# A list scheduler's figure for the speed of transfers: 280 bytes per ns in place of 240

## The chip, the core and the metric

One core of a Trainium2 chip runs the kernel. The metric is the device time of one execution in microseconds, and a lower time is better. TensorE (PE) does the matrix products, VectorE (DVE) and ScalarE (ACT) the elementwise work, GpSimd (POOL) and SyncE (SP) issue the transfers between the chip's main memory and its on-chip memory. Each engine works through its own instructions in the order in which they were written; an instruction whose input isn't there holds up all that stands behind it on that engine.

## What is computed

Attention with a compressed memory, and behind it a feed-forward layer with a squared relu, all in fp32 accuracy.

```python
a = softmax(phi, axis=2)                       # phi: 8 batches, 8 heads, 576 rows, 32 columns
k_m = einsum('bhsm,bhsd->bhmd', a, k)          # 32 memory rows of 64 numbers for each head
v_m = einsum('bhsm,bhsd->bhmd', a, v)
attn = softmax(q @ k_m.T / sqrt(64))           # 576 x 32 for each head
x = (attn @ v_m), heads side by side           # 4608 tokens x 512
g = relu(x @ w_in) ** 2                        # w_in 512 x 2048
out = g @ w_out                                # w_out 2048 x 512
```

## The kernel before

Every number that enters a product is split into a high and a low part, and a product is three products of parts. v_m is multiplied into w_in ahead of time, so that x is never formed: for each batch b and each of 16 slices of 128 columns of the hidden layer there is a step g (128 steps). **mm1** (L740) multiplies the attention with the prepared slice ("vw") into h; ACT or DVE apply the relu (L744, L745) and the square (L746 gives the high part gh, L748 the full square); DVE subtracts (L750) to get the low part **glo**. **mm2** adds gh (L770, L771) and then glo (L773) times w_out ("wo") into four accumulators.

The first 180 us also hold work that is done once. The 16 slices of w_in and w_out, two halves each, come encoded; `decode` turns a half into its parts. For each of these 32 halves it issues a load of 512 KB, **raw** (L322, on SP's queue), DVE reads that in L324 and L326 and goes on with L327, L328, L340 or L342, L344 and L357, ACT works in between (L325 and a copy), and for the first slices PE subtracts in L350, L351 and L352, of which the last needs what L340 wrote. POOL stores the parts of w_in to memory (L364), and adds the low part of w_out by a transfer (L361); `wi_again` loads the parts of w_in once more for other batches (L369). A raw buffer is loaded again when DVE has read it for the last time (L340 or L342). `memory` loads k, v and phi of four heads of a batch (L377, L378; two buffers of KV), makes the softmax of phi, and forms k_m and v_m on PE (**pkv**, L426). `scores` (L557 loads q, L569 transposes it on DVE) and `first_attention` (for batches 0 and 1; scores on PE in L636, back to rows in L664 and L671, low parts on DVE in L668) make the attention; its softmax is L682 to L688 on DVE.

The order of all of it is not written out by hand. `Plan.order` is a list scheduler: each operation has a duration for each engine that can do it, a list of what it must wait for, and, if it is a transfer, a size in bytes. A backward pass gives each operation a latest start; a forward pass fills the engines, always with the most urgent operation that is ready on the engine that is free first, and keeps one clock for all transfers, `wire`. Operations marked `lead` count as 9000 ns more urgent. The schedule sets the order on each engine (and, for a few operations that two engines can do, the engine). Where its times are off, the order stays, and the engine waits in that order. A transfer's time in the schedule is made so:

```python
wire = max(wire, t + 600) + o.size / WIRE
o.end = wire + LANDS[e]          # LANDS: 1400 ns for SP, 4000 for POOL
```

The size of a raw load is 4096 * 128 = 524,288 bytes.

Of the kernel before, what the change touches and what calls it, by code (L numbers as in the profile page):

```python
# [24 lines left out]

STEP = 5200
LANDS = {"SP": 1400, "POOL": 4000}
WIRE = 240.0
LEAD = 9000


# [21 lines left out]
class Plan:  # L53
# [56 lines left out]

    def order(self):
        for o in reversed(self.ops):
            cost = min(o.ways.values()) + o.lat + o.size / WIRE + (1800 if o.size else 0)
            late = min((u.late for u in o.users), default=1e9)
            if o.cap is not None:
                late = min(late, o.cap)
            o.late = late - cost
        for o in self.ops:
            o.left, o.ready = len(o.deps), 0.0
        free = {"PE": 0.0, "DVE": 0.0, "ACT": 0.0, "POOL": 0.0, "SP": 0.0}  # L120
        wire = 0.0
        port = {"DVE": 0.0, "POOL": 0.0}
        waiting = {e: [] for e in free}
        ready = {e: [] for e in free}

        def add(o):
            for e in o.ways:
                heapq.heappush(waiting[e], (o.ready, o.seq, o))

        for o in self.ops:  # L130
            o.start = None
            if not o.left:
                add(o)
        out = []
        while len(out) < len(self.ops):
            best = None
            for e in free:
                w, q = waiting[e], ready[e]
                while w and (w[0][0] <= free[e] or w[0][2].start is not None):
                    _, _, o = heapq.heappop(w)  # L140
                    if o.start is None:
                        heapq.heappush(q, (o.late - (LEAD if o.lead else 0), o.seq, o))
                while q and q[0][2].start is not None:
                    heapq.heappop(q)
                if q:
                    t = free[e]
                elif w:
                    t = w[0][0]
                else:
                    continue  # L150
                if best is None or t < best[0]:
                    best = t, e
            t, e = best
            free[e] = max(free[e], t)
            w, q = waiting[e], ready[e]
            while w and w[0][0] <= free[e]:
                _, _, o = heapq.heappop(w)
                if o.start is None:
                    heapq.heappush(q, (o.late - (LEAD if o.lead else 0), o.seq, o))
            while q and q[0][2].start is not None:  # L160
                heapq.heappop(q)
            if not q:
                continue
            _, _, o = heapq.heappop(q)
            t = free[e]
            d = o.ways[e]
            if o.port.get(e):
                other = "POOL" if e == "DVE" else "DVE"
                t = max(t, port[other])
                port[e] = t + d  # L170
            o.start, o.left = t, e
            free[e] = t + d
            o.end = t + d + o.lat
            if o.size:
                wire = max(wire, t + 600) + o.size / WIRE
                o.end = wire + LANDS[e]
            out.append(o)
            for u in o.users:
                u.left -= 1
                u.ready = max(u.ready, o.end)  # L180
                if not u.left:
                    add(u)
        out.sort(key=lambda o: (o.start, o.seq))
        return out
# [752 lines left out]
```

## Time and profile before

| | us |
|---|---|
| median of 3 timed runs | 819.76 |
| lowest and highest of these | 812.38 and 821.96 |
| the profiled execution's own time | 816.34 |
| its span, first to last instruction | 814.6 |

The profiled execution has 1.7 us outside its span, and its time lies inside the three timed ones. The mean granted TensorE clock is 0.994 of full speed. In rows of the profile, "idle" in square brackets is how long an engine had stood still before an instruction, and behind the arrow is what ended that.

### The profile page before, as it was taken

To read this page: it belongs to the slowest core of one execution; us is meant where nothing else is said; L and a number is where in the kernel's file an instruction comes from. 1 tells how busy PE (TensorE), PEld (TensorE's weight loads), DVE (VectorE), ACT (ScalarE), POOL (GpSimd) and SP (SyncE) were. 2 spreads that over 40 slices of the span, in tenths; PEclk is the share of its full clock that TensorE was granted. 3 is DMA by queue.
4 is the path that set the end of the run, shared out by engine and by line. 5 is a ranking of instruction groups with operands and counts; after the bars stand their busy time and mean duration, and the time that the engine had idled before them with its cause. 6 is when DMAs were issued, how large, how long until landed. Compare 5 with 4: busy or idle time off the path is not lost.

```text
span 814.6 us, 13267 instructions
## 1 busy us (share of the span) xinstructions
PE 776.2 (95%) x4926; PEld 652.5 (80%) x4926; DVE 536.4 (66%) x1190; ACT 403.1 (49%) x922; POOL 63.8 (8%) x103
## 2 busy tenths in 40 slices
PE   4889999999999999999999999999999999999995
PEld 2567888778887888888778888888788888888884
DVE  4678888783468976766776556877677556864540
ACT  2557766675653465634445355644334355643220
POOL 4012202320100100010000100010000100000000
PEclk9999999999999999999999999999999999999998
DMA  7969967666456523423443433513422433100001
GB/s 225 270 191 286 270 176 239 188 170 191 125 146 189 165 81 105 129 37 90 132 125 88 126 106 104 136 34 91 133 58 70 122 108 104 30 24 29 1 1 64
DMA packets 99716, 101.04 MB, mean 124 GB/s; under 512 B 32260, under 2 KB 85508, under 8 KB 99652
## 3 DMA queue, kind: packets, MB, share of 16 engines
q1 hardware_dynamic: 89188, 81.55, 34.2%
q0 software_dynamic: 10464, 18.65, 8.8%
q8 instruction: 39, 0.64, 0.3%
q14 instruction: 25, 0.20, 0.1%
HBM read 79.17 MB, written 17.83 MB: 119 GB/s over the span
## 4 chain that ended last, share of the span: by engine, by line
PE 73%; DVE 8%; issue 6%; DMA 5%; ACT 4%; SPq 1%; POOL 1%; DVEq 0%; POOLq 0%; ACTq 0%
PE h L740 20%; PE acc L770 12%; PE acc L773 12%; PE acc L771 12%; PE accl L796 5%; PE pvw L536 4%; PE psc L574 3%; PE pkv L426 2%; DMA raw<-in_moe_w_out_dram 1%; DMA phi<-in_phi_dram 1%; ACT vw L260 1%; DMA raw<-in_moe_w_in_dram 1%; DMA wo<-work 1%; DVE glo L750 1%; DVE work L327 1%
## 5 line engine op out<-in xcount | busy, mean ns | idle before, releaser
L740 PE MATMUL h<-ath,vw 128*128 128x320 f32 (+1 forms) x1024 | 211.6, 298 | 1.1 <-ACT r L744 0.6
L770 PE MATMUL acc<-wo,gh 128*128 128x512 f32 x512 | 207.0, 404 | 1.8 <-ACT gh L746 1.6
L771 PE MATMUL acc<-wo,gh 128*128 128x512 f32 x512 | 201.7, 394 | 0.0
L740 PEld LDWEIGHTS h<-ath,vw 128*128 128x128 f32 x1024 | 171.0, 189 | 17.2 <-ACT r L744 1.7
L773 PE MATMUL acc<-wo,glo 128*128 128x512 f32 x512 | 162.1, 405 | 1.7 <-DVE glo L750 1.5
L260 ACT CAST vw<-pvw 64x256 fp32r<-64x256 f32 (+1 forms) x224 | 85.7, 397 | 74.5 <-PE pvw L536 35.4
L545 DVE TENSOR_TENSOR vw<-pvw,vw 64x256 fp32r<-64x256 f32 x192 | 78.8, 420 | 64.8 <-ACT vw L260 62.9
L770 PEld LDWEIGHTS acc<-wo,gh 128*128 128x128 f32 x512 | 96.4, 188 | 23.4 <-ACT gh L746 3.7
L740 PE MATMUL h<-atl,vw 128*128 128x320 f32 (+1 forms) x512 | 109.9, 295 | 0.0
L771 PEld LDWEIGHTS acc<-wo,gh 128*128 128x128 f32 x512 | 96.4, 188 | 16.6
L773 PEld LDWEIGHTS acc<-wo,glo 128*128 128x128 f32 x512 | 89.5, 189 | 19.5 <-DVE glo L750 6.2
L746 ACT ACTIVATE gh<-r 128x512 fp32r<-128x512 f32 x128 | 80.8, 632 | 43.4 <-DVE r L745 37.6
L750 DVE TENSOR_TENSOR glo<-r,gh 128x512 fp32r<-128x512 f32 x128 | 87.5, 684 | 21.4 <-ACT r L748 19.7
L744 ACT ACTIVATE r<-h 128x256 f32<-128x256 f32 (+1 forms) x149 | 60.1, 406 | 56.8 <-PE h L740 53.5
L745 DVE TENSOR_SCALAR r<-h 128x320 f32<-128x320 f32 (+1 forms) x107 | 48.9, 459 | 58.4 <-PE h L740 57.9
L740 PEld LDWEIGHTS h<-atl,vw 128*128 128x128 f32 x512 | 82.5, 189 | 0.7 <-issue 0.2
L747 ACT ACTIVATE gl<-r 128x64 fp32r<-128x64 f32 x128 | 32.8, 256 | 68.5 <-DVE r L745 66.5
L748 ACT ACTIVATE r<-r 128x576 f32<-128x576 f32 x94 | 64.5, 686 | 2.2
L796 PE MATMUL accl<-wo,gl 128*128 128x512 f32 x192 | 52.3, 397 | 0.1
L796 PEld LDWEIGHTS accl<-wo,gl 128*128 128x128 f32 x192 | 35.0, 188 | 7.2 <-DVE o L260 0.5
L536 PE MATMUL pvw<-wi,VTh 128*128 128x256 f32 x192 | 37.3, 286 | 0.6 <-issue 0.3
L749 DVE TENSOR_TENSOR r<-r 128x576 f32<-128x576 f32 x34 | 25.7, 756 | 15.8 <-ACT gh L746 14.4
(137 smaller groups left out, 854.3 us busy)
## 6 DMA issues: line engine op xcount, KB each, us to landing
wi<-w_in_hi SPq DMA_DIRECT2D x56, 256.0 KB
wi<-w_in_lo SPq DMA_DIRECT2D x56, 256.0 KB
KV<-in_k_dram SPq DMA_DIRECT2D x32, 256.0 KB
KV<-in_v_dram SPq DMA_DIRECT2D x32, 256.0 KB
raw<-in_moe_w_in_dram SPq DMA_DIRECT2D x16, 512.0 KB
raw<-in_moe_w_out_dram SPq DMA_DIRECT2D x16, 512.0 KB
q<-in_q_dram SPq DMA_DIRECT2D x24, 288.0 KB
out_dram<-o POOLq DMA_DIRECT2D x20, 256.0 KB, 7.7
```

What stands on the lines that cost most here:

```text
L260: nc.scalar.copy(o, i) if e == "ACT" else ENG[e].tensor_copy(o, i)
L536: nc.tensor.matmul(pw()[:, x * SL:(x + 1) * SL], l()[:, 2 * hh + x, :], w(r, x), start=(i == 0), stop=(i == 2))
L545: vec({"DVE": tt(SL)}, lambda e, V=V, pr=pr, src=src: nc.vector.tensor_sub(V()[pr, 1, hh, :], src(), V()[pr, 0, hh, :].bitcast(F32)), [pw, ...
L740: nc.tensor.matmul(p()[:, 0:n], V()[:, l, hh, c0:c0 + P], x()[:, hh, cs], start=(i == 0), stop=(i == 5))
L744: op({"ACT": act(n) - 30, **({} if b < 2 else {"DVE": tt(n)})}, lambda e, cs=cs, n=n, p=p: nc.scalar.activation(r()[:, cs], p()[:, 0:n], A ...
L746: op({"ACT": act(SM)}, lambda e: nc.scalar.activation(gh(), r()[:, 0:SM], AF.Square), [r], [gh])
L748: op({"ACT": act(S), **({} if b < 2 else {"DVE": tt(S)})}, lambda e: nc.scalar.activation(r(), r(), AF.Square) if e == "ACT" else nc.vecto ...
L750: vec({"DVE": tt(SM)}, lambda e: nc.vector.tensor_sub(glo(), r()[:, 0:SM], gh().bitcast(F32)), [r, gh], [glo])
L770: nc.tensor.matmul(a(), gh()[:, c], t()[:, 0], start=f0, stop=False)
L771: nc.tensor.matmul(a(), gh()[:, c], t()[:, 1], start=False, stop=False)
L773: nc.tensor.matmul(a(), glo()[:, c], t()[:, 0], start=False, stop=f1)
L796: nc.tensor.matmul(a(), G()[:, l, :], t()[:, w], start=(ff == 0 and n == 0), stop=(ff == NFF - 1 and n == 2))
```

## The change

The one figure becomes two: 240 for transfers that the forward pass places in the first 30,000 ns of its own time, 280 for those after, and 280 for all in the backward pass. No operation is added or removed, no buffer and no size changes.

```diff
-WIRE = 240.0
+WIRE = (240.0, 280.0)
...
-            cost = min(o.ways.values()) + o.lat + o.size / WIRE + (1800 if o.size else 0)
+            cost = min(o.ways.values()) + o.lat + o.size / WIRE[1] + (1800 if o.size else 0)
...
-                wire = max(wire, t + 600) + o.size / WIRE
+                wire = max(wire, t + 600) + o.size / WIRE[t > 30000]
```

A raw load is 2185 ns of the scheduler's wire at 240 and 1872 at 280. What it does to the program is another order: on PE some 256 of its 1629 runs of like instructions stand elsewhere, 11 of 283 transfers on SP's queue, 3 of 94 on POOL's; 68 operations go from ACT to DVE or back (DVE has 10 more, ACT 10 fewer). The first difference lies near 37 us of the time before; most lie between 60 and 290, some between 340 and 450 and between 540 and 650; the last 150 us are the same.

**SP's queue, near 62 us.** KV_1_1 holds half of k and v of batch 1, and raw is the load of half a slice of w_in. Before:

```order
L377 DMA KV_1_1_631<-in_k_dram 128x2x256
L378 DMA KV_1_1_631<-in_k_dram 64x2x64
L377 DMA KV_1_1_631<-in_v_dram 128x2x256
L378 DMA KV_1_1_631<-in_v_dram 64x2x64
L322 DMA raw<-in_moe_w_in_dram 128x2x512
```

and now:

```order
L377 DMA KV_1_1_633<-in_k_dram 128x2x256
L378 DMA KV_1_1_633<-in_k_dram 64x2x64
L322 DMA raw<-in_moe_w_in_dram 128x2x512
L377 DMA KV_1_1_633<-in_v_dram 128x2x256
L378 DMA KV_1_1_633<-in_v_dram 64x2x64
```

The raw load has gone ahead of the two loads of v.

**DVE, near 86 us.** glo_1004 and glo_1005 are step 3's, wi_3_1 is half a slice of w_in that is being decoded, L324 begins the decoding of a half of w_out, and red and S belong to the softmax of batch 1. Before:

```order
L750 TENSOR_TENSOR glo_1004<-r_950,gh_971 128x512
L328 TENSOR_SCALAR work<-work 128x512
L682 TENSOR_REDUCE red_0_1012<-S_0_1002 128x16
L340 SCALAR_TENSOR_TENSOR wi_3_1_1006<-raw,work 128x512
L324 TENSOR_SCALAR work<-raw 128x512
L326 TENSOR_SCALAR work<-raw 128x512
L683 TENSOR_TENSOR S_0_1002<-S_0_1002,red_0_1012 128x512
```

and now:

```order
L750 TENSOR_TENSOR glo_1005<-r_956,gh_977 128x512
L328 TENSOR_SCALAR work<-work 128x512
L324 TENSOR_SCALAR work<-raw 128x512
L340 SCALAR_TENSOR_TENSOR wi_3_1_953<-raw,work 128x512
L326 TENSOR_SCALAR work<-raw 128x512
L751 TENSOR_TENSOR gl_992<-r_956,gl_992 128x64
L327 SCALAR_TENSOR_TENSOR work<-work 128x512
```

L324 now stands ahead of L340 of wi_3_1, and the softmax has gone behind (its L682 is 7 rows further on).

**PE at the same place.** psc are the scores of batch 1, pd is what decoding puts on PE. Before:

```order
L350 MATMUL pd_0_998<-work,ident 128x512
L636 MATMUL psc_0_973<-kbd_0_652,qT_0_859 128x64 x8
L351 MATMUL pd_0_998<-wi_3_0_968,minus 128x512
L352 MATMUL pd_0_998<-wi_3_0_968,minus 128x512
L770 MATMUL acc_0_3_617<-wo_686,gh_971 128x512
L771 MATMUL acc_0_3_617<-wo_686,gh_971 128x512
L636 MATMUL psc_1_1021<-kbd_1_842,qT_1_907 128x64 x8
L350 MATMUL pd_1_1038<-work,ident 128x512
L351 MATMUL pd_1_1038<-wi_3_1_1006,minus 128x512
L352 MATMUL pd_1_1038<-wi_3_1_1006,minus 128x512
L773 MATMUL acc_0_0_555<-wo_686,glo_1004 128x512
```

and now:

```order
L352 MATMUL pd_0_947<-wi_3_0_900,minus 128x512
L613 MATMUL pq_1_1_966<-ident,q_1_386 128x128 x4
L740 MATMUL h_1_1081<-ath_449,vw_0_2_889 128x320 x2
L350 MATMUL pd_1_987<-work,ident 128x512
L351 MATMUL pd_1_987<-wi_3_1_953,minus 128x512
L622 MATMUL pql_996<-ident,qx_427 128x128 x2
L352 MATMUL pd_1_987<-wi_3_1_953,minus 128x512
L773 MATMUL acc_0_0_555<-wo_662,glo_1005 128x512
L773 MATMUL acc_0_1_606<-wo_662,glo_1005 128x512
L740 MATMUL h_0_1095<-ath_449,vw_0_2_889 128x256
L636 MATMUL psc_0_1019<-kbd_0_658,qT_0_876 128x64 x4
```

Both blocks of psc stood ahead of L352 of wi_3_1, and now stand behind it.

**DVE, near 133 us.** glo_1545 and glo_1534 are step 10's, glo_1570 is step 11's, and the last L324 in the first piece reads the load for a half of w_out. Before:

```order
L328 TENSOR_SCALAR work<-work 128x512
L342 SCALAR_TENSOR_TENSOR work<-raw,work 128x512
L324 TENSOR_SCALAR work<-raw 128x512
L750 TENSOR_TENSOR glo_1545<-r_1506,gh_1522 128x512
L751 TENSOR_TENSOR gl_856<-r_1506,gl_856 128x64
L344 TENSOR_TENSOR work<-work 128x512
```

and now:

```order
L327 SCALAR_TENSOR_TENSOR work<-work 128x512
L750 TENSOR_TENSOR glo_1534<-r_1479,gh_1512 128x512
L751 TENSOR_TENSOR gl_940<-r_1479,gl_940 128x64
L328 TENSOR_SCALAR work<-work 128x512
L342 SCALAR_TENSOR_TENSOR work<-raw,work 128x512
L750 TENSOR_TENSOR glo_1570<-r_1536,gh_1546 128x512
L344 TENSOR_TENSOR work<-work 128x512
L751 TENSOR_TENSOR gl_992<-r_1536,gl_992 128x64
L324 TENSOR_SCALAR work<-raw 128x512
```

The low parts of steps 10 and 11 stood behind that L324, and now stand ahead of it.

## Rows read from the trace of the kernel before

**Rows 1.** The profile page, busy time of each engine.

```profile
PE 776.2 (95%) x4926; PEld 652.5 (80%) x4926; DVE 536.4 (66%) x1190; ACT 403.1 (49%) x922; POOL 63.8 (8%) x103
```

**Rows 2.** The page, the chain that ended last, by engine.

```profile
PE 73%; DVE 8%; issue 6%; DMA 5%; ACT 4%; SPq 1%; POOL 1%; DVEq 0%; POOLq 0%; ACTq 0%
```

**Rows 3.** Busy us in five stretches; last PEclk, DMA share, GB/s.

```profile
0.00:60.00 60.00, 41.95 (x405) 28.52 (x406) 36.24 (x85) 27.59 (x56) 13.74 (x26) 0.97 0.81 228
60.00:130.00 70.00, 68.07 (x467) 56.23 (x466) 59.15 (x128) 50.41 (x108) 14.76 (x20) 1.00 0.84 250
130.00:200.00 70.00, 64.75 (x383) 56.24 (x382) 49.94 (x99) 46.60 (x100) 14.32 (x18) 1.00 0.66 189
200.00:260.00 60.00, 59.42 (x453) 48.73 (x453) 33.57 (x80) 30.31 (x70) 3.51 (x9) 1.00 0.53 149
260.00:815.00 555.00, 542.02 (x3227) 462.77 (x3225) 357.48 (x801) 248.15 (x590) 17.49 (x31) 0.99 0.30 86
```

**Rows 4.** The same columns, 20 us each, where transfers are densest.

```profile
60.00:80.00 20.00, 19.57 (x171) 14.80 (x170) 16.19 (x37) 13.83 (x30) 3.48 (x7) 1.00 0.90 288
80.00:100.00 20.00, 20.00 (x130) 16.68 (x129) 18.19 (x39) 15.93 (x35) 6.36 (x8) 1.00 0.92 260
```

**Rows 5.** Waits of PE, 60 to 200 us: total us, times, longest.

```profile
PE pvw L516 <- ACT vw L260: 2.0, 2, 1.6
PE acc L770 <- ACT gh L746: 1.6, 2, 0.9
PE patl L671 <- DVE atl L668: 1.5, 1, 1.5
PE acc L773 <- DVE glo L750: 1.3, 1, 1.3
PE pd L352 <- DVE wi L340: 0.4, 1, 0.4
```

**Rows 6.** Waits of DVE for transfers, the same stretch and columns.

```profile
DVE work L324 <- DMA wo<-work: 6.3, 3, 3.1
...
DVE work L324 <- DMA raw<-in_moe_w_out_dram: 3.5, 3, 1.4
...
DVE work L324 <- DMA raw<-in_moe_w_in_dram: 1.5, 3, 0.8
```

**Rows 7.** Timeline near 62 us: start, us, engine, line.

```profile
62.17 0.64 SPq L377 DMA_DIRECT2D KV<-in_v_dram  x1
...
64.50 0.37 SPq L322 DMA_DIRECT2D raw<-in_moe_w_in_dram  x1
...
69.32 0.54 PE L426 MATMUL pkv<-KV,phi 128*32 128x128 f32 x12
```

**Rows 8.** Timeline of SP, PE and DVE, 81 to 91 us.

```profile
81.83 3.77 SPq L322 DMA_DIRECT2D raw<-in_moe_w_out_dram  x2
...
84.85 1.96 PE L636 MATMUL psc<-kbd,qT 128*128 128x64 f32 x16
...
86.61 0.48 PE L351 MATMUL pd<-wi,minus 128*128 128x512 f32 x1
...
87.63 1.89 PE L636 MATMUL psc<-kbd,qT 128*128 128x64 f32 x16
88.07 0.68 DVE L340 SCALAR_TENSOR_TENSOR wi<-raw,work 128x512 fp32r<-128x512 uint32 x1
...
89.43 0.55 DVE L324 TENSOR_SCALAR work<-raw 128x512 f32<-128x512 f32 x1 [0.68 <-DMA raw<-in_moe_w_out_dram]
...
90.50 0.39 PE L352 MATMUL pd<-wi,minus 128*128 128x512 f32 x1
```

**Rows 9.** Timeline of PE, 108 to 111 us.

```profile
109.13 0.33 PE L671 MATMUL patl<-ident,S 128*128 128x128 f32 x1 [1.49 <-DVE atl L668]
```

**Rows 10.** Timeline of DVE, 128 to 136 us.

```profile
133.78 0.43 DVE L324 TENSOR_SCALAR work<-raw 128x512 f32<-128x512 f32 x1 [1.44 <-DMA raw<-in_moe_w_out_dram]
134.12 0.68 DVE L750 TENSOR_TENSOR glo<-r,gh 128x512 fp32r<-128x512 f32 x1
```

**Rows 11.** Timeline of PE at the same place.

```profile
134.86 0.73 PE L773 MATMUL acc<-wo,glo 128*128 128x512 f32 x2 [1.33 <-DVE glo L750]
```

**Rows 12.** Timeline of SP, DVE and PE, 184 to 199 us.

```profile
185.06 0.55 SPq L557 DMA_DIRECT2D q<-in_q_dram  x1
...
190.13 0.69 DVE L750 TENSOR_TENSOR glo<-r,gh 128x512 fp32r<-128x512 f32 x1 [0.83 <-ACT r L748]
...
192.75 0.60 SPq L557 DMA_DIRECT2D q<-in_q_dram  x1
...
196.71 0.71 DVE L569 STREAM_TRANSPOSE qT<-q 128x512 f32<-128x512 f32 x1 [4.33 <-DMA q<-in_q_dram]
...
198.34 0.62 PE L773 MATMUL acc<-wo,glo 128*128 128x512 f32 x2
```

## The prediction

> **What bounds the kernel now.** I began with the busy time of each engine: PE is busy for 776 of 815 us, DVE for 66%, ACT for 49% [rows 1]. The chain that ended last agrees, with PE on 73% of it [rows 2]. A share over the whole span hides stages, so the table of five stretches came next [rows 3]. Before 60 us PE stands for 60.00 - 41.95 = 18.1 us. Then it stands for 1.9 us up to 130, 5.3 us from 130 to 200, 0.6 us from 200 to 260, and 13.0 us in the 555 us after that. After 60 us, then, PE is the bound by its work, and the change leaves that work as it is: the same products, in another order. A new order can only take away PE's waits or make new ones. There are 7.2 us of PE idle between 60 and 200 us to take away. A new wait there costs its full length, since later stretches have too little idle time in which to make it up.
>
> Who holds PE up in that stretch is in the waits: ACT with vw (2.0 us) and gh (1.6), DVE with atl (1.5), glo (1.3) and L340 (0.4) [rows 5]. DVE in turn stood 11.3 us at L324, the first reader of a raw load or of a buffer that a transfer must free (6.3 + 3.5 + 1.5) [rows 6]. Only 1.3 us of that came through to PE, in a place that I come to below.
>
> Is the new figure nearer the truth? Where transfers are densest they moved 288 and 260 GB/s at a busy share of 0.90 and 0.92 [rows 4], which divided by the share is 320 and 283. As a rate of the whole, 280 describes this better than 240. But the schedule needs something else: when one load is there. A raw load of 524,288 bytes is 2.2 us of its wire at 240 and 1.9 at 280, plus 0.6 before and 1.4 behind, so 4.2 and then 3.9 us if nothing is ahead of it. The load issued at 81.83 was waited for until 89.43, which is 7.6 us [rows 8]. At that place the old figure was already too hopeful, and the new one is more so.
>
> **The change, place by place.** All sums are against the profiled execution, 816.34 us.
>
> *Near 62 us, SP.* The raw load moves ahead of the two loads of v. It waited for a buffer until 64.50, so the loads of v that began at 62.17 now begin at 64.87: 2.7 us later [rows 7]. PE used them at 69.32 without idle time of its own, so they had landed by then; how long before, these rows don't say. The cost to PE is 0 to 2.7 us. Which value it is doesn't matter much, because the next place swallows it.
>
> *Near 88 us, DVE and PE.* L324 of the next half of w_out now stands ahead of L340 of wi_3_1. In the trace L324 could only start at 89.43, when its load was there, while L340 had gone at 88.07 [rows 8]. The load is issued when DVE frees its buffer, and that part of DVE's row keeps its place, so I keep 89.43. L340 then starts behind L324's 0.55 us and takes 0.68: it ends at 90.66. On PE, L352 needs L340's result. In the trace PE came to it at 90.50 with two blocks of scores ahead of it; they took 86.61 - 84.85 = 1.76 and 89.36 - 87.63 = 1.73 us [rows 8]. Both are now behind, so PE comes to L352 at 90.50 - 3.49 = 87.01 and waits until 90.66: **+3.6 us**, and a delay from 62 us shortens this wait by as much as it lasted. The bounds are 0 (the load comes 3.6 us sooner, since its buffer is free sooner) and +4.5 (the load shares its time with more others). I take 3.6, since it is built on the rows of this very load.
>
> *95 to 115 us.* The scores of batch 1 come later, and with them the softmax and the return to rows (L671). PE's wait there, 1.5 us [rows 9], was a wait for atl at a time when DVE had too much to do. PE now comes 3.6 us later with more filler ahead (steps 5 to 7 and the next slices of vw move up), in the new order that chain stands behind four to five us more of DVE's work; the two about match, so I count the wait as gone: **-1.5**, bounds -1.5 and +2. The low part of step 4 stands behind a further L324, whose load is issued late by the same lag; I add **+0.5**, bounds 0 and +3 (the 3.1 us that was the longest wait of an L324 [rows 6]).
>
> *Near 133 us, DVE.* The low part of step 10 stood behind an L324 that waited 1.44 us for its load, and PE waited 1.33 us for that low part [rows 10, 11]. It now stands ahead of the L324: **-1.3**, bounds -1.3 and 0. What is late next there is L344 behind the same L324, which feeds the decoding and not PE.
>
> *Near 190 us, DVE.* L569, which waits for q, moves ahead of the low part of step 20. It stood 4.3 us for q in the trace, the second part of which was issued at 192.75; this part now goes directly behind the first, at about 185.6 [rows 12]. At the 4.0 us or less that it took (192.75 to 196.71) it is there at 189.6, and at the 7.6 that the raw load of rows 8 took, at 193.2. L569 (0.7), a maximum of about twice that, and the subtraction itself (0.7) then put the low part of step 20 at 196.0 at the latest. PE needs it at 198.34 [rows 12]. The cover is 2.3 us, so **0**; without it, up to +2.
>
> *The rest.* The waits for ACT, 3.6 us in all [rows 5], may go or double: 0, bounds -3.6 and +3.6. After 200 us steps of `memory` for batches 2 to 4 move 6 to 10 us of PE's work ahead, in a stretch where PE stands for 0.6 us [rows 3]; it is filler that changes places: 0, bounds -3 and +3.
>
> The sum is 3.6 - 1.5 + 0.5 - 1.3 = +1.3, so 817.6 for an execution like the profiled one. The median of the timed runs lies 3.4 us above that execution and would give 821.1. Three runs that spread over 9.6 us don't say which is the better zero, so I take the middle: **819 us**.
>
> The Trainium skill, page "DMA: Bandwidth & Descriptors", section "Queues, rings and completion order", says that each of the 16 engines takes turns, packet by packet, between all queues that have work for it. By this rule no single queue of transfers with one rate tells when a load lands, since a load is stretched by whatever POOL and SP have under way beside it, and a hopeful figure puts DVE in front of an absent load again and again. The trace agrees at one place: 524,288 bytes in 7.6 us are 69 bytes per ns for this load [rows 8], while all transfers together moved 260 GB/s [rows 4]. By the figure of the schedule (3.9 us) the place near 88 us would cost nothing and the sum would be 814 us; by the rule it costs 3.6 or more, and the first rival below is its general form.
>
> **The rivals.**
>
> *Slower.* DVE works in order, and each L324 that comes ahead of its load holds up the low parts, L340 and softmaxes behind it. Some 22 raw loads are still to come after 60 us. If the block of 88 us came at five more of them, at about 2.7 us each that come through to PE, that is 3.6 + 13.5 - 2.8 = +14.3: 831 us. It decides where DVE has less other work between an L324 and its load than the load is late. For it: DVE is busy for 18.19 of 20 us near 90 us [rows 4], so it can't catch up there, and loads took 7.6 us. Against it: of 11.3 us that DVE stood at L324, PE felt 1.3 [rows 5, 6], because PE has mostly other work queued.
>
> *Faster.* 280 is the truer rate, waits go and few come: the 7.2 us of PE idle between 60 and 200 shrink to nothing, 816.34 - 7.2 = 809 us. For it: the rate [rows 4], and two waits that I see going. Against it: the waits for ACT are no matter of transfers. More than 2% would need the 18 us before 60 us as well, and there the order is nearly the same until 37 us.
>
> *Nothing.* The order differs, but PE is the bound and the differences are filler: 816 to 820 us. It is told from my forecast by the trace alone: no new wait at L352 near 88 us, and the one at 134.86 still there.
>
> **How the numbers follow.** My forecast, gain and loss that nearly cancel, gets 0.38; nothing 0.28; the faster rival 0.22; the slower one 0.12. The range takes 808 (just under the faster rival) and 831 (the slower one), and leaves out some 0.1 at each side for the bounds that add up (-1.5 - 1.3 - 3.6 - 3 gives 807; 4.5 + 2 + 3 + 3.6 on 819.76 gives 833). Two per cent, about what a measurement of this kernel can tell from no change, is 16.4 us: below 803 or above 836. The faster rival comes that far only with part of the first 60 us, 0.05; the slower one with seven or more such blocks, 0.09; the rest, 0.86, lies within.
>
> **What would show it.** In the changed kernel's profile, PE should wait 2 to 4 us at L352 near 88 to 91 us with L340 named, and L324 should be idle for a raw load just ahead of that. The wait of L671 near 109 should be gone or below 0.5 us, and so should that of L773 for glo near 135. pkv near 69 us should begin later or wait. L569 should follow q at 190 to 193 us, and PE shouldn't wait for glo there. PE's idle time from 200 us on should be what it was. I am wrong if the load is there by 86 us (then 814 or less), or if several L324 hold PE up between 95 and 180 us (then 826 or more).

## The result, and the profile after

The changed kernel's median is 822.36 us (820.57 to 830.84, 20 runs) against 817.89 (812.38 to 823.83, 20 runs) for the kernel before on the same chip: ratio 1.0073, 95% interval 1.0044 to 1.0103. The ratio goes by the means of the runs, which lie 6.0 us apart; the medians lie 4.5 apart. That is within 2%, as forecast, but it is a loss of 4.5 to 6 us, clear of noise, and not the +1.3 of the sum. The profiled execution took 822.78 us, its span 821.0; before it was 816.34 and 814.6.

The page of the changed kernel, busy time and the chain by engine [rows 1, 2]:

```profile
PE 779.0 (95%) x4926; PEld 654.9 (80%) x4926; DVE 542.4 (66%) x1200; ACT 397.8 (48%) x912; POOL 63.4 (8%) x103
...
PE 71%; DVE 9%; issue 7%; DMA 6%; ACT 3%; POOL 1%; SPq 1%; DVEq 0%; POOLq 0%; ACTq 0%
```

PE was idle for 814.6 - 776.2 = 38.4 us before and for 821.0 - 779.0 = 42.0 now: 3.6 us of the 6.4 between the spans are new idle time, and 2.8 are the same 4926 matmuls at longer times. The chain agrees: PE 71% in place of 73%, the difference at DVE, DMA and issue. Not all of the 6.4 us can come from the change: ahead of 37 us, where the first row differs, the changed kernel's execution is already 1.4 us behind, as the first block of scores shows (before, then now):

```profile
26.80 2.00 PE L636 MATMUL psc<-kbd,qT 128*128 128x64 f32 x16
```

```profile
28.21 2.00 PE L636 MATMUL psc<-kbd,qT 128*128 128x64 f32 x16
```

The stretches of [rows 3] and the 20-us windows of [rows 4], in the changed kernel:

```profile
60.00:130.00 70.00, 64.70 (x445) 52.74 (x444) 53.80 (x119) 47.65 (x101) 12.04 (x16) 1.00 0.83 244
130.00:200.00 70.00, 65.56 (x383) 57.34 (x382) 54.09 (x107) 47.00 (x100) 17.21 (x22) 0.98 0.65 186
...
80.00:100.00 20.00, 16.73 (x109) 13.17 (x107) 14.98 (x33) 12.65 (x26) 6.00 (x8) 1.00 0.89 248
```

The new idle time is between 60 and 130 us: 1.93 us before, 5.30 now. Nearly all of that is the window from 80 to 100 us, where PE had been busy throughout. What PE waited for from 60 to 200 us, and VectorE for loads in the same stretch [rows 5, 6]:

```profile
PE pvw L524 <- ACT vw L260: 3.5, 2, 2.0
PE pd L352 <- DVE wi L340: 3.3, 2, 2.0
PE acc L773 <- DVE glo L750: 1.5, 2, 1.2
PE pkv L426 <- DMA KV<-in_v_dram: 0.6, 1, 0.6
```

```profile
DVE work L324 <- DMA raw<-in_moe_w_out_dram: 6.3, 4, 2.7
...
DVE work L324 <- DMA raw<-in_moe_w_in_dram: 5.3, 3, 2.5
...
DVE work L324 <- DMA wo<-work: 2.9, 1, 2.9
```

The waits of L324 for raw loads have grown from 3.5 + 1.5 to 6.3 + 5.3 us. The timeline near 88 us of the changed kernel [rows 8] shows how they come through (start, duration, engine, line, idle ahead):

```profile
80.98 0.37 SPq L369 DMA_DIRECT2D wi<-w_in_hi  x1
81.46 0.44 SPq L322 DMA_DIRECT2D raw<-in_moe_w_in_dram  x1
...
83.23 5.14 SPq L322 DMA_DIRECT2D raw<-in_moe_w_out_dram  x2
...
86.31 0.43 DVE L324 TENSOR_SCALAR work<-raw 128x512 f32<-128x512 f32 x1 [2.50 <-DMA raw<-in_moe_w_in_dram]
87.32 0.69 DVE L340 SCALAR_TENSOR_TENSOR wi<-raw,work 128x512 fp32r<-128x512 uint32 x1
88.06 0.50 PE L352 MATMUL pd<-wi,minus 128*128 128x512 f32 x1 [1.96 <-DVE wi L340]
...
91.05 0.43 DVE L324 TENSOR_SCALAR work<-raw 128x512 f32<-128x512 f32 x1 [1.50 <-DMA raw<-in_moe_w_out_dram]
91.39 0.68 DVE L340 SCALAR_TENSOR_TENSOR wi<-raw,work 128x512 fp32r<-128x512 uint32 x1
92.13 0.50 PE L352 MATMUL pd<-wi,minus 128*128 128x512 f32 x1 [1.31 <-DVE wi L340]
```

The second wait, 1.31 us, is the forecast's place: L340 of wi_3_1 behind L324 of the half of w_out. The first, 1.96 us, was not foreseen. It has the same form one half earlier: L340 of wi_3_0 (87.32) stands behind L324 of wi_3_1 (86.31), whose load is late. That load, the raw load of wi_3_1, now stands on SP behind a reload (L369) that waits for its store, so it was issued at 81.46; in the profile before, the pair of w_in loads to which it belongs began at 75.99 and was issued by 79.4.

The second group of waits runs through ScalarE. Near 178 us:

```profile
178.37 0.43 DVE L324 TENSOR_SCALAR work<-raw 128x512 f32<-128x512 f32 x1 [2.67 <-DMA raw<-in_moe_w_out_dram]
178.83 0.63 ACT L325 ACTIVATE work<-work 128x512 f32<-128x512 f32 x1 [3.53 <-DVE work L324]
179.37 0.57 ACT L260 CAST vw<-pvw 128x512 fp32r<-128x512 f32 x1
...
179.99 0.71 PE L524 MATMUL pvw<-vw,minus 128*128 128x512 f32 x1 [1.99 <-ACT vw L260]
...
180.50 0.73 PE L740 MATMUL h<-ath,vw 128*128 128x320 f32 x2
```

ScalarE's L325 belongs to the same decode as L324. It stands ahead of the cast of vw that L524 needs, so a load that is late for VectorE holds ScalarE and then PE. The wait of 1.52 us at 153.96 has the same form, but there L324 stands for a transfer (wo<-work, 2.93 us) that must free its buffer, and not for a load. Behind the wait at 179.99 the clock fell, as the 2-us windows show (the column after POOL is the granted clock):

```profile
178.00:180.00 2.00, 0.01 (x1) 0.01 (x1) 1.63 (x5) 1.17 (x3) 0.00 (x0) 1.00 0.06 25
180.00:182.00 2.00, 2.00 (x7) 1.89 (x8) 2.00 (x5) 1.51 (x4) 0.00 (x0) 0.53 0.00 0
182.00:184.00 2.00, 2.00 (x11) 1.81 (x10) 2.00 (x5) 1.25 (x3) 0.28 (x1) 0.62 0.80 248
184.00:186.00 2.00, 2.00 (x13) 1.76 (x12) 1.38 (x5) 1.03 (x3) 1.59 (x3) 1.00 0.49 94
```

The execution before has such a fall too, at another place, so this one needn't be a net loss of the changed kernel:

```profile
44.00:46.00 2.00, 2.00 (x6) 1.01 (x5) 2.00 (x5) 1.27 (x3) 0.12 (x1) 0.50 1.02 244
```

### The profile page after: what moved, and what is told of

It is laid out like the page before. It is cut to its first block, busy times and chain, and to the rows that moved or that the text cites. A ratio compares the mean times of both kernels' runs of the same rounds, so it can differ in the third digit from the quotient of the medians.

```text
span 821.0 us, 13261 instructions
## 1 busy us (share of the span) xinstructions
PE 779.0 (95%) x4926; PEld 654.9 (80%) x4926; DVE 542.4 (66%) x1200; ACT 397.8 (48%) x912; POOL 63.4 (8%) x103
## 4 chain that ended last, share of the span: by engine, by line
PE 71%; DVE 9%; issue 7%; DMA 6%; ACT 3%; POOL 1%; SPq 1%; DVEq 0%; POOLq 0%; ACTq 0%
PE h L740 19%; PE acc L770 12%; PE acc L771 12%; PE acc L773 11%; PE accl L796 5%; PE pvw L536 4%; DMA raw<-in_moe_w_in_dram 2%; PE psc L574 2%; PE pkv L426 2%; DVE mx L409 1%; DMA phi<-in_phi_dram 1%; DVE glo L750 1%; DMA KV<-in_v_dram 1%; ACT vw L260 1%; DMA raw<-in_moe_w_out_dram 1%
## 5 line engine op out<-in xcount | busy, mean ns | idle before, releaser
L740 PE MATMUL h<-ath,vw 128*128 128x320 f32 (+1 forms) x1024 | 215.2, 299 | 1.1 <-ACT ath L667 0.7
L770 PE MATMUL acc<-wo,gh 128*128 128x512 f32 x512 | 204.5, 399 | 0.5 <-ACT gh L746 0.2
L773 PE MATMUL acc<-wo,glo 128*128 128x512 f32 x512 | 161.2, 406 | 1.9 <-DVE glo L750 1.9
L770 PEld LDWEIGHTS acc<-wo,gh 128*128 128x128 f32 x512 | 96.7, 189 | 20.0 <-ACT gh L746 1.4
L740 PE MATMUL h<-atl,vw 128*128 128x256 f32 (+1 forms) x512 | 110.6, 297 | 0.0
L773 PEld LDWEIGHTS acc<-wo,glo 128*128 128x128 f32 x512 | 89.1, 188 | 19.8 <-DVE glo L750 5.9
L747 ACT ACTIVATE gl<-r 128x64 fp32r<-128x64 f32 x128 | 32.7, 255 | 60.4 <-DVE r L745 58.0
L748 ACT ACTIVATE r<-r 128x576 f32<-128x576 f32 x84 | 57.5, 685 | 1.8
L749 DVE TENSOR_TENSOR r<-r 128x576 f32<-128x576 f32 x44 | 33.2, 755 | 17.7 <-ACT gh L746 15.9
```

What stands on the lines that cost most here:

```text
L740: nc.tensor.matmul(p()[:, 0:n], V()[:, l, hh, c0:c0 + P], x()[:, hh, cs], start=(i == 0), stop=(i == 5))
L748: op({"ACT": act(S), **({} if b < 2 else {"DVE": tt(S)})}, lambda e: nc.scalar.activation(r(), r(), AF.Square) if e == "ACT" else nc.vecto ...
L770: nc.tensor.matmul(a(), gh()[:, c], t()[:, 0], start=f0, stop=False)
L773: nc.tensor.matmul(a(), glo()[:, c], t()[:, 0], start=False, stop=f1)
```

## The experiments

All are timed against the kernel before on one chip per group. Its medians there were 813.58 us (first group), 814.62, 813.52 and 815.18.

**Repairing the places.** The program's build sorts the emitted rows once more, so an edit of the plan alone doesn't fix the order. These kernels hold the named operations behind others; 534 and 535 are the reload, 362 the raw load of wi_3_1, 368 its L340, and 380 and 382 the L324 and L326 of the half of w_out. e2 has the second pair alone, e3 both. The traces show that e1 moved one load on SP's queue and nothing else, while in e2 and e3 the second sort also moved rows at 19 places on PE and 12 on ScalarE.

```diff
+    ran, after = {}, {534: 362, 535: 362}                      # e1; e2: {380: 368, 382: 368}
     for o in plan.order():
-        o.fn(o.left)
+        with (tc.issue_after(ran[after[o.seq]].ins) if o.seq in after else ExitStack()): ran[o.seq] = o.fn(o.left)
```

e1, expected:

> The changed kernel, with one place on SP's queue put back: both reloads of w_in's first slice stand behind the raw load of wi_3_1 again, as before the change. Theory one (SP stood 5.4 us at the reload, the raw load behind it came late, DVE stood 2.5 us at its L324, PE 1.96 us at L352 near 88 us): that raw load is issued 2 to 5 us sooner, the L352 wait at 88 us falls under 0.5 us, and the time is 1 to 2 us lower than the changed kernel's (by its profile 821.0 us of span: 819 to 820). Rival (PE's waits only move, since the load after it is the later one): the L352 wait near 92 us grows by as much, and the span stays within 0.5 us.

Measured: 820.69 us, 1.0076 (1.0045 to 1.0106).

e2, expected:

> The changed kernel, with one place on DVE put back: L324 and L326 of the half of w_out stand behind L340 of wi_3_1 again. Theory one (PE waited 1.31 us at L352 near 92 us, because L340 stood behind an L324 without its load): this wait goes, the one at 88 us (1.96) stays, span 1 to 1.5 us lower. Rival (DVE is the bound there, the wait comes back at glo of step 4 or at the softmax): the wait of L773 near 107 us grows from 1.2 to over 2 us and the span stays.

Measured: 823.82 us, 1.0129 (1.0086 to 1.0172).

e3, expected:

> Both places put back, on SP and on DVE. Theory one: both L352 waits go, 3.3 us of PE, and the span falls by 2.5 to 3.5 us to about 818; the time lands at 1.003 of the kernel before. Rival (what is saved near 90 us is lost again by 200 us): the span falls by less than 1 us.

Measured: 822.75 us, 1.0104 (1.0069 to 1.0138).

e4 holds L324 to L326 of every decode in the plan's own order, which moves rows at 72 places on PE:

```diff
-        o.fn(o.left)
+        i = o.fn(o.left); (o.fn.__code__.co_firstlineno in (324, 325, 326)) and tc.keep_in_program_order(i)
```

> The changed kernel, with L324, L325 and L326 of all decodings kept where the list schedule put them, so that the build can't let them float ahead of rows whose input is there. Theory one (all five waits of PE above 1 us between 80 and 200 us have an L324 without its data ahead on DVE, or an L325 behind such an L324 ahead on ACT): these waits, 8.0 us in the changed kernel, fall to 3 us or less, and the span falls by 3 to 6 us, to the kernel before or below. Rival one (decoding then comes too late, and PE waits for decoded parts at L350 to L352, L516 or L770 in place): the span is the changed kernel's or up to 10 us longer. Rival two (most of the loss lies after 200 us): the span falls by less than 2 us though the waits go.

Measured: 821.17 us, 1.0087 (1.0057 to 1.0117).

The theory that those few places hold the loss isn't borne out: no repair brought time back. Neither is it refuted, since e2 to e4 are other orders in much else too. In e3 neither wait of L352 is left, but L516 waits 1.8 us at the same place for ScalarE and 2.1 us for vw later. In e1 the first wait at L352 went and the one at the forecast's place grew from 1.31 to 1.95 us, and the clock fell behind it:

```profile
88.70 0.50 PE L352 MATMUL pd<-wi,minus 128*128 128x512 f32 x1 [1.95 <-DVE wi L340]
...
95.03 3.51 PE L636 MATMUL psc<-kbd,qT 128*128 128x64 f32 x16
```

```profile
88.00:90.00 2.00, 1.30 (x8) 1.17 (x9) 1.78 (x5) 1.92 (x5) 0.00 (x0) 1.00 1.01 404
...
94.00:96.00 2.00, 2.00 (x12) 2.00 (x11) 1.59 (x4) 1.20 (x3) 0.71 (x1) 0.50 0.93 240
```

Sixteen L636 take 3.51 us here and 1.96 at full clock [rows 8]. The granted clock stayed near 0.50, the lower of the two levels (1.2 GHz), from about 90 to 100 us; 10 us of PE's work at half the clock are some 5 us by estimate, more than the wait itself. In e3 it fell at the same place, behind the wait of L516, and stayed at 0.50 to 0.55 from 90 to 104 us: some 7 us by the same estimate, twice the waits that the repair took away.

**Which pass, or any move of the figure?**

```diff
-WIRE = 240.0
+WIRE = (240.0, 280.0)    # e5: [1] in the backward pass alone; e6: [t > 30000] in the forward pass alone
+WIRE = 242.0             # e7, everywhere; e8: 220.0
```

e5, expected:

> Edit: 280 only in the backward pass that sets the latest times; the forward pass keeps 240 everywhere. Theory A (the figure of the forward pass in the dense part of 30 to 200 us makes the loss, because rows are placed there as if their transfers had landed): this run has the time of before, ratio 0.998 to 1.003, no wait of PE over 1.5 us between 80 and 180 us. Theory B (the backward pass, which alone moves rows after 340 us, makes the loss): ratio 1.004 to 1.010, and the mm2 instructions of 340 to 460 us fall back by about 2 us more against before, as in the changed kernel. Theory C (the order of before is a favourable one and any move of it costs): also slow, 1.004 to 1.012.

Measured: 823.4 us (one of its eight runs, 833.56, lies apart; 822.38 without it), 1.0094 (1.0063 to 1.0126).

e6, expected:

> Edit: 280 only in the forward pass after 30 us; the backward pass keeps 240. Theory A: ratio 1.005 to 1.010, with waits of PE of 1 to 2 us for L340 or for the casts of vw between 80 and 180 us behind an L324 that waits for its load. Theory B: 0.998 to 1.003, and no new lag between 340 and 460 us. Theory C: 1.004 to 1.012, with the waits at other places than in the changed kernel.

Measured: 826.23 us, 1.0124 (1.0081 to 1.0168).

e7, expected:

> Edit: the single figure 242 in place of 240 in both passes, a change of under 1% in every transfer's estimate, which still reorders about a tenth of VectorE's rows in the first third of the program. Theories A and B: the estimate is the same to 1%, so the time is that of before, ratio 0.997 to 1.003. Theory C: the order of before is a favourable draw and this one another draw: 1.004 to 1.012, with waits of PE over 1 us at places of its own.

Measured: 819.06 us, 1.0056 (1.0033 to 1.0079).

e8, expected:

> Edit: the single figure 220 in place of 240, a slower estimate, moved the other way than the change. Theory A says that a slower estimate is the safer side (rows that use a load are placed later): ratio 0.993 to 1.002, fewer waits of VectorE for transfers than before. Theory C: 1.004 to 1.012, as slow as the changed kernel, although the figure was moved the other way.

Measured: 823.96 us, 1.0108 (1.007 to 1.0145).

A laid the loss to the figure of the forward pass, B to that of the backward pass, C to any move away from a favourable order. This speaks for C against A and B: each of these four moves costs 0.6 to 1.2%, whichever way the figure goes, even by 1%. The profile of e5 showed a disturbance that is no matter of waits. Here are rows of it, its window from 20 to 40 us, and the same L350 in the kernel before:

```profile
20.77 2.05 PE L350 MATMUL pd<-work,ident 128*128 128x512 f32 x2 [0.15 <-DVE work L327]
...
32.05 3.67 PE L636 MATMUL psc<-kbd,qT 128*128 128x64 f32 x16
```

```profile
20.00:40.00 20.00, 18.77 (x139) 14.35 (x140) 7.26 (x20) 6.15 (x12) 2.39 (x4) 1.00 0.99 276
```

```profile
20.03 1.10 PE L350 MATMUL pd<-work,ident 128*128 128x512 f32 x2 [0.30 <-DVE work L327]
```

PE's matmuls are twice as long in e5 up to 39 us, and in the kernel before only up to 19, though the clock column says 1.00 for both. The column can't be read there: the trace's record of the clock begins at 39.3 us in e5 and at 19.4 in the kernel before, with the upper level, and the column counts what lies ahead of the record as 1.00. The Trainium skill, "TensorE: Matmul & The Clock Gate", section "Seeing it yourself", calls the recorded clock events unreliable on trn2. No run here shows a wrong entry; what misleads is the stretch ahead of the first one, with L636 at 3.67 us under a column of 1.00.

**Controls, and the forecast's place by itself.** e9 is the kernel before, unchanged. e10 is the kernel before with L340 (368) behind the L326 (382) of the half of w_out, and nothing else moved. e11 and e12 are the kernels before and after with idle matmuls in PE's early waits; nothing is left out, and the second sort moves rows at some 12 places on VectorE and 8 on ScalarE with them.

```diff
+    ran, after, todo = {}, {368: 382}, plan.order(); todo.insert(417, todo.pop(412))      # e10
...
+    for _ in range({("wi", 0, 0): 14}.get((kind, j, h), 0)): nc.tensor.matmul(pd()[:, 0:P], ident, ident, start=True, stop=True)   # e11, e12
```

e9, expected:

> Edit: none, the kernel before once more under a name of its own, as a control of the comparison and for a second profile. Every variant so far took 0.6 to 1.2% longer than before, in whichever way the figure was moved. Theory C (a comparison that favours the kernel it is made against, or an order of before that is a lucky draw): the first half of it says 1.004 to 1.010 here too. All others say 0.997 to 1.003. Theory D (TensorE goes over from its lower level to the higher one at a time that differs between executions, 20 to 38 us in the profiles so far, L350 x2 at 2.05 against 1.10 us): the profile of this run may have the rise at another time than 20 us, with the identical order.

Measured: 813.41 us, 1.000 (0.9971 to 1.0029).

e10, expected:

> Edit: the kernel before with one place alone taken from the changed kernel: L340 of wi_3_1 stands behind L324 and L326 of the half of w_out near 88 us; every other row keeps its place. The forecast's first term: TensorE waits 3 to 4 us at L352 near 91 us and the run is 3 to 4 us longer (ratio 1.003 to 1.005). Rival (the wait is caught up by 120 us, as the changed kernel's lag against before fell from 5.5 at 100 us to 3.1 at 140): 0 to 2 us, 0.998 to 1.003. Theory C (any move costs a draw): 1.004 to 1.012.

Measured: 813.2 us, 0.999 (0.9957 to 1.0022).

e11, expected:

> Edit: the kernel before with 14 more matmuls of ident by ident (128x128) into the bank of the first L350, whose results L350 overwrites; they fill the waits of TensorE between 6 and 15 us. Theory D: TensorE is at its higher level from about 15 us in every execution; L350 x2 near 15 to 20 us at 1.10 us; median 0 to 3 us under before and the spread of the times narrower than 812 to 819 (ratio 0.996 to 1.000). If the late rise has nothing to do with the idle time of TensorE: ratio 1.000 to 1.004 and a rise at 20 us or later.

Measured: 812.02 us, 0.9974 (0.9946 to 1.0003).

e12, expected:

> Edit: the changed kernel with the same 14 matmuls. Theory A (the forward figure's waits of 80 to 180 us make the loss) with theory D: the early part is the same as in the warmed kernel before, and the changed kernel stays 4 to 6 us behind it: ratio to before 1.003 to 1.006. Theory D alone (the loss is the late rise): equal to the warmed kernel before, 0.996 to 1.002. If filling does nothing: 1.007 to 1.010, as the changed kernel.

Measured: 821.92 us, 1.0099 (1.0068 to 1.013).

The comparison has no bias that e9 shows. PE's waits from 60 to 200 us in e9, with the same order as before, and its window from 100 to 140:

```profile
PE pvw L516 <- ACT vw L260: 1.6, 1, 1.6
PE acc L770 <- ACT gh L746: 1.2, 2, 0.7
PE pd L352 <- DVE wi L340: 0.4, 1, 0.4
PE pvw L524 <- ACT vw L260: 0.3, 1, 0.3
```

```profile
100.00:140.00 40.00, 39.93 (x238) 35.06 (x237) 34.77 (x73) 29.76 (x66) 7.44 (x10) 1.00 0.74 226
```

L671 and L773, which waited 1.5 and 1.3 us in the profile before [rows 5, 9, 11], don't wait here, and not in e10 either, where PE's order is that of before row by row. These waits belonged to one execution, not to the order. The two executions of the one program, e9 and before, differ by 5.7 us of PE's idle time (808.5 - 775.8 = 32.7 in place of 38.4), more than the 3.6 us above. And PE's busy time is 780.4 us in e10, 4.2 more than before with the same matmuls in the same order, so the changed kernel's 2.8 us more needn't come from its order.

In e10 VectorE's rows stand as the forecast priced them (with L326 ahead of L340 too), and the load is late as it said; but PE's two blocks of scores still stand ahead of L352, as in the kernel before (timeline of VectorE and PE, L340 and L352 of wi_3_1):

```profile
92.15 1.90 PE L636 MATMUL psc<-kbd,qT 128*128 128x64 f32 x16
...
94.11 0.43 DVE L324 TENSOR_SCALAR work<-raw 128x512 f32<-128x512 f32 x1 [1.44 <-PE psc L636]
...
94.78 0.69 DVE L340 SCALAR_TENSOR_TENSOR wi<-raw,work 128x512 fp32r<-128x512 uint32 x1
...
95.53 0.50 PE L352 MATMUL pd<-wi,minus 128*128 128x512 f32 x1 [0.33 <-DVE wi L340]
```

L324 stood 1.44 us. The view names L636, which ended the wait last, but by the trace the load's last piece came only 0.05 us sooner, at 94.01; it had been issued at 86.65, 7.4 us earlier. PE waited 0.33 us. By the forecast's own working that is what this half of the swap should cost: L340 ends at 90.66 and PE, with the scores ahead, comes at 90.50. So the 3 to 4 us expected of e10 left out that the other half, the scores behind L352, wasn't in it, and e10 doesn't test the forecast's first term. It shows that the half on VectorE costs nothing in the median while PE has the scores to do.

The idle matmuls did what D says in e11 (two L350 take 1.02 us at 17.30) and not in e12 (1.75 us at 17.49). There the record has the upper level from 10.8 us, PE waits 3.54 us at 17.25, and the granted clock is 0.50 from 18 to 20 us. So D in the form "in every execution" fell. At the first block of scores e12 is 1.5 us behind e11 (27.64 and 26.15 us), and in the medians the two kernels stay 9.9 us apart, so the early level isn't the main cause of that.

**One part at a time.** All with the same 14 matmuls.

```diff
+ ... o.size / WIRE[1]                      # e13, e14, e15: the backward pass; e16 has 240 there
+ ... o.size / WIRE[30000 < t < 130000]     # e14, forward; e15: [t > 130000]; e16: [t > 30000]; e13 has 240 there
```

e13, expected:

> Edit: 280 in the backward pass only, with the 14 idle matmuls. Theory A (the forward figure's waits make the loss; the backward kernel was slow by the late rise of TensorE's level alone): as the warmed kernel before, ratio 0.996 to 1.001. Theory B (the backward pass carries it): 1.006 to 1.010, as the changed kernel warmed. Theory C (each redraw of the order costs its own waits): between, or above, 1.003 to 1.010, with its lag at other places than the changed kernel's.

Measured: 821.96 us, 1.0082 (1.0049 to 1.0114).

e14, expected:

> Edit: 280 in the backward pass, and in the forward pass from 30 to 130 us of the plan only, with the 14 idle matmuls. Theory A, its first half (the loads of 80 to 100 us: TensorE at L352 near 88 and 92 us): the run is 3 to 4 us over the backward-only one, ratio 1.002 to 1.006, with the wait at L352 of 2 us or more near 88 us. Theory B or C: within 2 us of the backward-only one, whichever that is.

Measured: 821.89 us, 1.0077 (1.0052 to 1.0102).

e15, expected:

> Edit: 280 in the backward pass, and in the forward pass behind 130 us of the plan only, with the 14 idle matmuls. Theory A, its second half (the casts of vw that stand behind L324 and L325 near 154 and 180 us): 1 to 3 us over the backward-only one, ratio 0.998 to 1.004, with the waits of L524 for vw in it. Theory B or C: within 2 us of the backward-only one.

Measured: 816.72 us, 1.0023 (0.9998 to 1.0047).

e16, expected:

> Edit: 280 in the forward pass behind 30 us only, with the 14 idle matmuls. Theory A: as the changed kernel warmed, ratio 1.005 to 1.010, with the wait of 2 to 4 us at L352 near 88 us. Theory B: 0.996 to 1.001, as the warmed kernel before. Theory C: 1.003 to 1.010 with waits at other places.

Measured: 822.71 us, 1.0087 (1.0059 to 1.0114).

VectorE's waits for raw loads from 60 to 140 us, and the window from 80 to 100, in e14 and then in e15:

```profile
DVE work L324 <- DMA raw<-in_moe_w_out_dram: 4.8, 3, 3.0
DVE work L324 <- DMA raw<-in_moe_w_in_dram: 4.6, 2, 2.4
```

```profile
80.00:100.00 20.00, 18.11 (x102) 14.08 (x101) 15.74 (x35) 12.63 (x27) 5.75 (x7) 0.91 0.87 257
```

```profile
DVE work L324 <- DMA raw<-in_moe_w_out_dram: 0.9, 1, 0.9
```

```profile
80.00:100.00 20.00, 19.91 (x129) 16.87 (x128) 17.82 (x38) 15.84 (x34) 6.29 (x8) 1.00 0.90 266
```

The same two views for the kernels of 240 and 280, sorted by the forward figure between 30 and 130 us:

| kernel | forward, 30 to 130 us | L324 for raw loads, 60 to 140 us | PE busy of 20 us, 80 to 100 | ratio |
|---|---|---|---|---|
| before; e9; e11 | 240 | 2.5; 1.0; 1.9 | 20.00; 20.00; 19.74 | 1; 1.000; 0.9974 |
| e5; e13 | 240 | 1.8; 2.2 | 19.48; 19.70 | 1.0094; 1.0082 |
| e15 | 240 | 0.9 | 19.91 | 1.0023 |
| after; e12 | 280 | 8.5; 8.3 | 16.73; 17.67 | 1.0073; 1.0099 |
| e14 | 280 | 9.4 | 18.11 | 1.0077 |
| e6; e16 | 280 | 8.0; 8.5 | 15.19; 17.04 | 1.0124; 1.0087 |

The first half of A is shown as far as the place goes: 280 in the forward pass from 30 to 130 us, and not in the other parts, makes 8 to 9.4 us of L324's waits in place of 1 to 2.5, and takes 2 to 5 us of PE's time between 80 and 100 us (242 and 220, e7 and e8, lie between, at 4.1 and 5.2 us). But the parts don't add. The backward pass alone loses as much without any of that (e13), the forward figure to 130 us adds nothing to it in the median (e14), and the one behind 130 us takes most of it away (e15, 5.2 us under e13). No theory expected that last one: A said 1 to 3 us above e13, B and C within 2 us of it. So the loss of an order as a whole isn't a sum of the loss of its parts, and C in the form "any move costs" fell as well: e15 and e10 show no cost clear of noise.

## Why the prediction was wrong

The forecast of 819 us against 819.76 was no change; the time rose by 0.73% (0.44 to 1.03).

**The credits of 2.8 us: the step that failed.** The waits at 109 and near 135 us went, as forecast, but e9 and e10 show that other executions with PE's order of before haven't got them. A wait that isn't in the order can't be taken out of it. Without these credits the sum is +4.1 us, a loss and not a draw.

**The term of +3.6 us: the mechanism was right, and the size in part by luck.** L352 waited 3.3 us in all, against 0.4, but at the forecast's place only 1.31. There L340 stood behind an L324 without its load, as the forecast said, and ended at 92.08; but PE came at 90.82 and not at 87.01, held up by the other 1.96 us and by what lay ahead of 88 us. The 1.96 came where a reload stands ahead of the raw load on SP, which the forecast didn't look for (with the reload put back, in e1, the forecast's place cost 1.95). The load of that place was issued at 83.23 and reached VectorE at 91.05, after 7.8 us, near the 7.6 of the working, while the schedule with 280 counts 0.6 + 1.9 + 1.4 = 3.9 us. Whether the two waits cost the kernel as much as they last isn't shown: e1 to e3 took them away in part or whole and gained nothing.

**The low part of step 4, +0.5 us:** L773 waited 1.17 us at 107.59, behind an L324 that stood 1.76 us for w_out. Mechanism right, size too small.

**Zero for ScalarE, with 3.6 to either side:** right in the sum, and not by its mechanism. L524's wait for vw rose from 0.3 to 3.5 us; L516 and L770 fell from 3.6 to 0.6. The step missed that L325 carries VectorE's wait on to ScalarE.

**PE's own time, put at nothing.** The sum has waits alone, and the profile has 2.8 us more of the same matmuls. As e10 shows, that much comes and goes while PE's order is the same, with the time at which the clock rises (19.4 us in the profile before, 23.1 in the changed kernel's, by the record).

**pkv, q and the end.** pkv waited 0.6 us, inside the 0 to 2.7. L569 waited 0.8 us for q, as forecast with no wait for glo. After 200 us PE's idle time was to stay, and it rose by 0.8 us (0.6 of it from 200 to 260), inside the 3.

**The middle.** The sum of +1.3 on one execution gave 817.6, and the forecast went halfway to the median, to 819: below the 819.76 it was to be compared with. By the 20 runs the median of the kernel before is 817.89, so halfway was near the right zero, by luck. On that zero the sum gives 819.2, and with the credits left out 822.0, close to the 822.36 measured. That nearness isn't proof: by e13 and e14 the loss doesn't add up place by place.

**The rivals.** The slower one had the right mechanism, repeated waits of L324, at a smaller size: between 60 and 200 us L324 stood 14.5 us for transfers in place of 11.3, and PE waited 8.3 us at L524, L352 and L773, most of it behind such an L324, where the forecast had counted 1.3 of the old ones. The sign that the forecast gave for it, several L324 that hold PE up between 95 and 180 us, came (107.59, 153.96 and 179.99), but at 822 us and not 826. The faster one took 280 for the truer rate; for when a load is there it isn't: with 280 in both passes the waits for raw loads doubled, from 5.0 to 11.6 us. But a slower figure, 220, was no better (e8).

**Open.** Why the backward pass alone costs 0.8%, and why the later forward figure takes most of that back, isn't settled. Against e11, e13 has 36.4 in place of 29.2 us of PE's idle time and 5.5 us more of PE's busy time, spread over many places. Part of that is the early level again (two L350 take 1.91 us at 17.69 in e13 and 1.02 at 17.34 in e15). PE's order is the same in e13 and e15 up to 157 us, so what sets their profiles apart before that, 2.8 us at the L524 of 153.58 and 150.74 us, is the execution's; the other 5.5 of the 8.3 us between their spans come behind it. The wait of L524 for vw (3.1 us in e13) doesn't decide it: e15 has the same 3.1 and loses little, and e14, as slow as e13, hasn't got it. That before is the fastest of ten orders (before, after, e1 to e8) is measured; whether a figure near 240 is better for a reason, or that order by luck, isn't. e11 is 0.26% under before, and its interval just reaches 1.

## What to carry to other kernels

Where a list schedule is this tight, a change of its constants is a redraw of the whole order: here seven other settings took 0.2 to 1.2% longer than the present one, and one of them had moved by 1%. So time the neighbours of a constant before believing a story about its truth. A row that consumes a load should be priced with the load's new issue time, by its queue, and with everything behind it on two engines, not one. A test of a swap needs both engines' halves of it. A credit for a wait that goes needs a second profile of the same program in which that wait is there too.

## What the hardware showed that wasn't expected

TensorE's two levels can cost as much as the waits. A wait of 2 us was followed by 4 us near the lower level in one place (0.53 and 0.62 at 180 to 184 us), by 10 us in another (e1, 90 to 100 us), and by none at 88 us of the changed kernel (e1's wait there was 1.95 us, the changed kernel's 1.96). At the program's start the record begins with the upper level at 19.4 us in the profile before and at 39.3 in e5, with nearly the same work: the second sixteen L636 began at 37.86 in e5 in place of 30.63 us. The Trainium skill, "TensorE: Matmul & The Clock Gate", section "HAM oscillation — how this bites in real kernels", tells of waits for loads after which matmuls run at the lower level; the trace agrees at the first two places and not at the third.
